# Attention and rational-activation FFN on one core: q and k of later units transposed with unrounded float32r bits and split after PSUM

## The chip, the cores and the metric

The kernel runs on one core of a Trainium2 chip. Its time is the device time of one execution in microseconds (us); a figure for a kernel is the median of several executions.

## The reference

Inputs: q, k and v of 4 batches, 8 heads, 768 positions, head size 64, all float32; weights w_in (512 x 2048) and w_out (2048 x 512); two small coefficient vectors a and b. Attention keeps the keys of a causal local window (`n_local` = 96) and the first `n_global` = 8 keys, with a linear distance bias per head; the output of the heads, 3072 tokens by 512, goes through a feed-forward layer with a rational activation.

```python
scores = scale * np.matmul(q, k.transpose(0, 1, 3, 2))
is_global = pos[None, :] < int(n_global)
is_local = (rel >= 0) & (rel < int(n_local))
keep = is_global | is_local
dist = np.where(is_global & ~is_local, float(n_local), np.abs(rel))
scores = np.where(keep, scores - slopes[:, None, None] * dist, -1e9)
a = softmax(scores);  attn = np.matmul(a, v)
...
h = x @ w_in
P = a[0] + a[1] * h + a[2] * h**2 + a[3] * h**3
Q = 1.0 + np.abs(b[0]) * np.abs(h) + np.abs(b[1]) * h**2
out = (P / (Q + 1e-06)) @ w_out
```

## The kernel before, in words

**Units and steps.** The work is cut into 96 units. A unit is one pair of heads of one tile of 128 queries; a chunk is 256 tokens (two tiles, eight units), and there are 12 chunks. `windowed` (L506) writes out a pipeline over steps t, 110 in all. At step t it emits, each with a priority (`PRI`, L42): the load of q, k and v for two units at every even step (`st_load`, L127), the transposes of unit t (`st_qkT`, L373), their eviction (`st_qkE`, L385), the split of unit t + 1 (`st_split`, L365), scores, softmax, normalization and copy of unit t - 2 (`st_score` L400, `st_soft` L424, `st_norm` L436, `st_raw` L446), the transposes of the probabilities of unit t - 3 (`st_pT`, L455), the product with v for a pair of units (`st_pv`, L468), and the feed-forward work of the slice that lies `LAG` = 12 steps back, its second product another `F2` = 2 steps later (`st_ffn1` L242, `st_ew1` to `st_ew4` L274 to L314, `st_ffn2` L320). In the first twenty-odd steps the weights are decoded from their 64-bit containers and split as well (`WSCHED`, `SPLITS`). A scheduler then puts each engine's instructions in a fixed order, by priority and by a simulated time of when each could run. On the chip each engine works through its list strictly in that order.

**Float32r products in parts.** The matmuls of the feed-forward layer and of the scores run in float32r, which keeps fewer bits, so each operand is split into a high part (rounded) and a low part (what rounding left). The feed-forward product of a slice takes three matmuls (high by high, high by low, low by high), on L258 and L334.

**q and k before the change.** A pair of units shares one tile `nat` of q and k (128 positions; 4 heads of 64). For a unit, `st_split` makes a tile `sp` with, for each head, the 64 high columns beside the 64 low columns: VectorE rounds (L369), GpSimd subtracts (L370). `st_qkT` transposes it on TensorE: four transposes of 128x128 (q and k, two heads) into one PSUM tile `tk` (L378), which after that has the high part of a head on partitions 0 to 63 and the low part on 64 to 127. `st_qkE` evicts it on ScalarE: q of each head with its scale (L392), k into the lasting tile `kT` (L395), for the first tile of a sequence also the global keys into `kG` (L397). Two DMAs on SyncE's queue copy q with the halves swapped (L393, L394), so that two matmuls per head (L408) sum all four products of parts.

**Queues and buffers.** All DMAs are issued by SyncE (SP), in order. The PSUM tiles of the transposes, the scores and the product with v (`tk`, `s`, `tp`, `o`) share one pool of three buffers. From unit `RAW` = 30 on, the normalized probabilities are copied by a DMA into a float32r tile with their bits unrounded (L452) and transposed in that form (L462); before unit 30 they are transposed as float32. The copy has one buffer.

The functions that the change touches:

Of the kernel before, what the change touches and what calls it, by code (L numbers as in the profile page):

```python
# [9 lines left out]
F32 = mybir.dt.float32  # L10
FR = mybir.dt.float32r
I32 = mybir.dt.int32
U16 = mybir.dt.uint16
AF = mybir.ActivationFunctionType
ALU = mybir.AluOpType
PSUM = bass.MemoryType.PSUM

P = 128
G = 8
# [3 lines left out]
TMPS = 6  # L23
GBUFS = 3
RAW = 30
LAG = 12
F2 = 2

# [67 lines left out]
def tile_kernel(ctx: ExitStack, tc: tile.TileContext, q, k, v, n_global, n_local,  # L96
                w_in, w_out, ca, cb, out):
    nc = tc.nc
    B, H, S, D = q.shape
# [15 lines left out]
    pl = SimpleNamespace(tmps=TMPS, gbufs=GBUFS, split=False)  # L115


    nat = {}
    vts = {}

    def unit(u):
        c, j = divmod(u, UPC)
        t, p = divmod(j, NPAIR)
        b, i = divmod(2 * c + t, NT)
        return c, t, p, b, i
# [81 lines left out]
    def split_w(key):  # L207
        low[key] = piece(FR, key)
        (nc.vector.tensor_copy if len(low) - 1 in HI_V else nc.scalar.copy)(out=w_hi(key), in_=full[key])
        (nc.vector if len(low) - 1 in LO_V else nc.gpsimd).tensor_tensor(  # L210
            out=low[key], in0=full[key], in1=w_hi(key), op=ALU.subtract)
# [137 lines left out]
    kT = const.tile([P, H, 2, P], FR, name="kT")  # L349
    kG = const.tile([P, H, G], FR, name="kG")  # L350
    ident = const.tile([P, P], F32, name="ident")
    ident_r = const.tile([P, P], FR, name="ident_r")
    mask0 = const.tile([P, P], F32, name="mask0")
    masks = const.tile([P, 3, P], F32, name="masks")
    sp = {}
    tqk = {}
    qTs = {}
# [4 lines left out]
    def blocks_of(x, i):  # L362
        return x if i else x[..., 0, :]

    def st_split(u):  # L365
        p = unit(u)[2]
        n = nat[u // 2][:, :, 2 * (p % 2):2 * (p % 2) + 2, :]
        s = pl.att.tile([P, 2, 2, 2, D], FR, tag="split", name=f"sp{u}", bufs=1)
        nc.vector.tensor_copy(out=s[:, :, :, 0, :], in_=n)  # L369
        nc.gpsimd.tensor_tensor(out=s[:, :, :, 1, :], in0=n, in1=s[:, :, :, 0, :], op=ALU.subtract)  # L370
        sp[u] = s

    def st_qkT(u):  # L373
        s = sp.pop(u)
        tk = pl.ps_t.tile([P, 2, 2, P], FR, tag="t", name=f"tk{u}")
        for z in range(2):
            for x in range(2):
                nc.tensor.transpose(out=tk[:, z, x, :], in_=s[:, z, x].rearrange("p a d -> p (a d)"),  # L378
                                    identity=ident_r)
        tqk[u] = tk  # L380
# [4 lines left out]
    def st_qkE(u):  # L385
        c, t, p, b, i = unit(u)
        tk = tqk.pop(u)
        hs = slice(2 * p, 2 * p + 2)
        qT = pl.att.tile([P, 2, 2, P], FR, tag="qT", name=f"qT{u}")
        for x in range(2):  # L390

            nc.scalar.activation(out=qT[:, 0, x], in_=tk[:, 0, x], func=AF.Copy, scale=float(2.0 ** (2 * p + x - 2)))  # L392
        nc.sync.dma_start(out=qT[0:D, 1].bitcast(F32), in_=qT[D:P, 0].bitcast(F32))  # L393
        nc.sync.dma_start(out=qT[D:P, 1].bitcast(F32), in_=qT[0:D, 0].bitcast(F32))  # L394
        nc.scalar.copy(out=kT[:, hs, i % 2, :], in_=tk[:, 1])  # L395
        if i == 0:
            nc.scalar.copy(out=kG[:, hs, :], in_=tk[:, 1, :, 0:G])  # L397
        qTs[u] = qT

    def st_score(u):  # L400
        c, t, p, b, i = unit(u)
        qT = qTs.pop(u)
        s_ps = pl.ps_t.tile([P, 2, 2, P], F32, tag="t", name=f"s{u}")
        for x in range(2):
            h = 2 * p + x
            rhs = kT[:, h] if i else kT[:, h, 0:1, :].broadcast_to([P, 2, P])
            for z in range(2):
                nc.tensor.matmul(out=s_ps[:, x], lhsT=qT[:, z, x, :], rhs=rhs, start=(z == 0), stop=(z == 1))  # L408
        if 1 <= i < NT - 1:
            nc.gpsimd.tensor_copy(out=kT[:, 2 * p:2 * p + 2, i % 2, 0:G], in_=kG[:, 2 * p:2 * p + 2, :])  # L410
        if i == 0:
            mk = mask0
        else:
            mk = masks[:, 0:2, :] if i % 2 else masks[:, 1:3, :]
        pr = pl.att.tile([P, 2, 2, P], F32, tag="prob", name=f"pr{u}")
        st = stats[:, u % 4]
        for x in range(2):
            h = 2 * p + x
            nc.vector.tensor_tensor_reduce(  # L419
                out=blocks_of(pr[:, x], i), in0=blocks_of(s_ps[:, x], i), in1=mk,  # L420
                scale=-(2.0 ** -(h + 1)), scalar=3e38, op0=ALU.add, op1=ALU.min, accum_out=st[:, x:x + 1])
        prob[u] = (pr, st)
# [23 lines left out]
    def st_raw(u):  # L446
        if u < RAW:
            return
        i = unit(u)[4]
        pr = prob[u][0]  # L450
        raw = pl.att.tile([P, 2, 2, P], FR, tag="raw", name=f"raw{u}", bufs=1)
        nc.sync.dma_start(out=blocks_of(raw.bitcast(F32), i), in_=blocks_of(pr, i))  # L452
        prob[u] = (raw, None)

    def st_pT(u):  # L455
        i = unit(u)[4]
        pr, st = prob.pop(u)
        W = 2 if i else 1
        t_ps = pl.ps_t.tile([P, 2, 2, P], FR if u >= RAW else F32, tag="t", name=f"tp{u}")
        for x in range(2):  # L460
            for w in range(W):
                nc.tensor.transpose(out=t_ps[:, x, w, :], in_=pr[:, x, w, :], identity=ident_r if u >= RAW else ident)  # L462
        pT = pl.att.tile([P, 2, 2, P], F32, tag="pT", name=f"pT{u}", bufs=2)
        t_ps = t_ps.bitcast(F32) if u >= RAW else t_ps
        (nc.scalar.copy if u < EARLY else nc.vector.tensor_copy)(out=pT[:, :, 0:W, :], in_=t_ps[:, :, 0:W, :])  # L465
# [40 lines left out]
    def windowed():  # L506
# [6 lines left out]
        nc.vector.tensor_copy(out=nf, in_=ni)  # L513
        load_coef()
        st_split(0)
        st_split(1)

        nl, ng = nf[:, 0:1], nf[:, 2:3]
# [4 lines left out]
        base = tc.cur_priority  # L523
        for t in range(NU + LAG + F2):
            f = t - LAG
            pri = PRI_A if f < FPC else PRI
# [9 lines left out]
            on("soft", st_soft, t - 2)  # L536
            on("ffn1a", st_ffn1, f, 0)
            on("qkT", st_qkT, t)
            if t % 2:
                on("pv", lambda u: st_pv(u // 2), t - 5)  # L540
            on("qkE", st_qkE, t)
            if t % 2:
                on("x", lambda u: st_x(u // 2), t - 5)
            if t:
                on("split", st_split, t + 1)
            if not is_last(f - 1):
                on("ew3", st_ew3, f - 1)
            on("norm", st_norm, t - 2)
            on("raw", st_raw, t - 2)
            if is_last(f):  # L550
                st_ew4(f - 1)
# [15 lines left out]
            for n, key in enumerate(list(full)[SPLITS.get(f - 1, 0):SPLITS.get(f, 0)]):  # L567
                tc.cur_priority = base + 1000 * t + pri["wsplit"] + 4 * n
                split_w(key)
        tc.cur_priority = base + 1000 * (NU + LAG + F2 + 4)  # L570

# [153 lines left out]
```

## Time and profile before

| | us |
|---|---|
| median of 3 runs | 794.35 |
| lowest, highest | 793.64, 794.79 |
| the profiled execution | 792.2 |
| its span, first to last instruction | 790.4 |

| engine | busy us | share of span |
|---|---|---|
| TensorE (PE), matmuls | 743.9 | 94% |
| TensorE, weight loads (PEld) | 649.6 | 82% |
| VectorE (DVE) | 599.6 | 76% |
| ScalarE (ACT) | 575.1 | 73% |
| GpSimd (POOL) | 533.3 | 67% |

In the profile, a row of a group of instructions has the line of the kernel, the engine and the operation; then the tile that is written `<-` the tiles that are read, the shape and the count; behind the first bar the busy time in us and the mean duration of one in ns; behind the second bar the idle time of that engine just before them, and what ended it. `PEld` is the load of weights for a matmul, which overlaps the matmul before it; `SPq` is SyncE's DMA queue. The page's digits show each of 40 equal slices of the span in tenths. Rows of a timeline or a chain begin with the start and the length in us.

### The profile page before, as it was taken

The page shows a single profiled execution, that of the slowest core. Times are in us where ns is not written, and L with a number is a line of the kernel's source. Part 1 is how long each engine was busy: PE and PEld are TensorE (multiplying, and loading weights), DVE is VectorE, ACT ScalarE, POOL GpSimd, SP SyncE. Part 2 cuts the span into 40 slices and gives each one's busy share as a digit, 9 for nine tenths or more (in the row PEclk, how much of TensorE's full clock was granted, in tenths as well). Part 3 has the DMA queues.
Part 4 walks back from the last instruction along what each step waited for, and adds up shares of the span by engine and source line. Part 5 has one row for each costly group of instructions (what it writes and reads, how often), then busy time and mean ns, then how long its engine had stood idle before and what let it go on. Part 6 is the DMA issues. An engine that isn't in the chain of part 4 may idle for free.

```text
span 790.4 us, 15799 instructions
## 1 busy us (share of the span) xinstructions
PE 743.9 (94%) x5184; PEld 649.6 (82%) x5184; DVE 599.6 (76%) x1453; ACT 575.1 (73%) x1407; POOL 533.3 (67%) x572
## 2 busy tenths in 40 slices
PE   3688978899999999999999999999999999999995
PEld 2467647688998899999899999989999999988993
DVE  5889999987778676777776786777677786776664
ACT  4778677667887777777777777777877777766763
POOL 3868558979877667666667667666677777664440
PEclk9999999899999999999999999999999999999999
DMA  7785445212222233333332332333332332210000
GB/s 183 212 240 173 114 125 189 49 48 54 55 81 68 85 92 87 97 88 86 82 87 82 106 84 81 106 84 82 88 85 77 101 92 78 82 55 14 28 1 32
DMA packets 111932, 72.19 MB, mean 91 GB/s; under 512 B 82912, under 2 KB 97248, under 8 KB 111840
## 3 DMA queue, kind: packets, MB, share of 16 engines
q1 hardware_dynamic: 111840, 71.08, 32.0%
q8 instruction: 44, 0.72, 0.4%
q14 instruction: 48, 0.39, 0.2%
HBM read 35.92 MB, written 6.29 MB: 53 GB/s over the span
## 4 chain that ended last, share of the span: by engine, by line
PE 81%; DVE 6%; POOL 5%; DMA 4%; issue 2%; ACT 1%; SPq 0%; DVEq 0%; POOLq 0%; ACTq 0%
PE h L258 32%; PE acc L334 31%; PE o L480 5%; PE s L408 5%; PE tp L462 3%; PE tk L378 3%; DMA r<-in_moe_w_in_dram 2%; POOL pr L441 2%; PE h L250 1%; POOL sp L370 1%; DMA nat<-in_k_dram 1%; POOL fa L291 1%; DVE pr L419 1%; DVE fu L305 0%; DMA r<-in_moe_w_out_dram 0%
## 5 line engine op out<-in xcount | busy, mean ns | idle before, releaser
L334 PE MATMUL acc<-wout_h,g 128*128 128x512 f32 x704 | 242.8, 403 | 0.8 <-ACT g L313 0.8
L258 PE MATMUL h<-xh,win_h 128*128 128x256 f32 x704 | 205.4, 292 | 1.8 <-DVE fu L290 1.8
L441 POOL TENSOR_SCALAR pr<-pr,stats 128x256 f32<-128x256 f32 (+1 forms) x192 | 178.5, 940 | 39.2 <-issue 12.7
L258 PE MATMUL h<-xl,win_h 128*128 128x256 f32 x704 | 198.7, 282 | 0.0
L291 POOL TENSOR_TENSOR fa<-fa,fs 128x512 f32<-128x512 f32 x95 | 125.1, 1317 | 100.7 <-ACT fs L284 97.4
L334 PEld LDWEIGHTS acc<-wout_h,g 128*128 128x128 f32 x704 | 126.6, 188 | 21.8 <-ACT g L313 1.2
L258 PEld LDWEIGHTS h<-xh,win_h 128*128 128x128 f32 x704 | 133.3, 189 | 10.9 <-issue 6.2
L258 PEld LDWEIGHTS h<-xl,win_h 128*128 128x128 f32 x704 | 133.3, 189 | 2.3 <-issue 0.2
L429 ACT ACTIVATE pr<-pr,stats 128x256 f32<-128x256 f32 (+1 forms) x192 | 93.5, 492 | 53.5 <-DVE stats L419 53.4
L370 POOL TENSOR_TENSOR sp<-nat,sp 128x256 fp32r<-128x256 f32 x96 | 75.8, 790 | 73.5 <-DVE stats L432 41.0
L314 POOL TENSOR_TENSOR g<-fu,g 128x512 fp32r<-128x512 f32 x87 | 112.7, 1295 | 7.7 <-DVE fu L290 4.6
L282 ACT ACTIVATE fu<-h,coef 128x512 f32<-128x512 f32 (+1 forms) x97 | 75.4, 778 | 54.1 <-PE h L258 49.6
L303 DVE SCALAR_TENSOR_TENSOR fu<-fu,coef,q 128x512 f32<-128x512 f32 (+1 forms) x97 | 71.6, 738 | 36.2 <-ACT q L299 35.0
L298 ACT ACTIVATE fs<-fa,coef 128x512 f32<-128x512 f32 (+1 forms) x97 | 70.2, 724 | 30.3 <-POOL fa L291 27.9
L289 DVE TENSOR_TENSOR fu<-fu,h 128x512 f32<-128x512 f32 (+1 forms) x97 | 65.6, 677 | 16.9 <-ACT fs L284 14.9
L465 DVE COPY pT<-tp 128x512 f32<-128x512 f32 (+1 forms) x75 | 48.5, 646 | 35.7 <-PE tp L462 35.0
L369 DVE CAST sp<-nat 128x256 fp32r<-128x256 f32 x96 | 38.3, 399 | 46.7 <-PE tk L378 15.1
L290 DVE SCALAR_TENSOR_TENSOR fu<-fu,coef,h 128x512 f32<-128x512 f32 (+1 forms) x97 | 71.7, 739 | 2.5
L419 DVE CUSTOM_DVE_ANT_0 pr<-s,masks 128x256 f32<-128x256 f32 x160 | 61.4, 420 | 15.2 <-PE s L408 13.3
L408 PE MATMUL s<-kT,qT 128*128 128x256 f32 x384 | 70.5, 305 | 1.8 <-DMA qT<-qT 1.7
L304 DVE SCALAR_TENSOR_TENSOR q<-fa,coef,q 128x512 f32<-128x512 f32 (+1 forms) x97 | 72.1, 744 | 0.0
L408 PEld LDWEIGHTS s<-kT,qT 128*128 128x128 f32 x384 | 61.5, 203 | 9.0 <-DMA qT<-qT 1.9
(273 smaller groups left out, 1658.8 us busy)
## 6 DMA issues: line engine op xcount, KB each, us to landing
raw<-pr SPq DMA_DIRECT2D x58, 256.0 KB
qT<-qT SPq DMA_DIRECT2D x192, 64.0 KB
r<-in_moe_w_in_dram SPq DMA_DIRECT2D x16, 512.0 KB
r<-in_moe_w_out_dram SPq DMA_DIRECT2D x16, 512.0 KB
nat<-in_q_dram SPq DMA_DIRECT2D x48, 128.0 KB
nat<-in_k_dram SPq DMA_DIRECT2D x48, 128.0 KB
vt<-in_v_dram SPq DMA_DIRECT2D x48, 128.0 KB
out_dram<-o SPq DMA_DIRECT2D x24, 256.0 KB
```

The costliest lines, as they stand in the source:

```text
L258: nc.tensor.matmul(out=hps[f][:, y, :], lhsT=w[:, fs], rhs=x[:, ct, :], start=(n == 0), stop=(n == 3 * NCT - 1))
L282: nc.scalar.activation(out=u, in_=h, func=AF.Identity, scale=a3, bias=a2)
L290: nc.vector.scalar_tensor_tensor(out=u, in0=u, scalar=a1, in1=h, op0=ALU.add, op1=ALU.mult)
L291: side(f).tensor_tensor(out=a, in0=a, in1=s, op=ALU.add)
L303: nc.vector.scalar_tensor_tensor(out=u, in0=u, scalar=a0, in1=r, op0=ALU.add, op1=ALU.mult)
L304: nc.vector.scalar_tensor_tensor(out=r, in0=a, scalar=q1, in1=r, op0=ALU.add, op1=ALU.mult)
L314: side(f).tensor_tensor(out=g[:, 1, ys], in0=u, in1=g[:, 0, ys], op=ALU.subtract)
L334: nc.tensor.matmul(out=acc, lhsT=gs[f][:, z, y, ts], rhs=w, start=(ft == 0 and n == 0), stop=(ft == NFT - 1 and n == 2))
L370: nc.gpsimd.tensor_tensor(out=s[:, :, :, 1, :], in0=n, in1=s[:, :, :, 0, :], op=ALU.subtract)
L408: nc.tensor.matmul(out=s_ps[:, x], lhsT=qT[:, z, x, :], rhs=rhs, start=(z == 0), stop=(z == 1))
L429: nc.scalar.activation(out=d, in_=d, func=AF.Exp, scale=-1.0, bias=st[:, x:x + 1], accum_out=st[:, 2 + 2 * x:3 + 2 * x])
L441: nc.gpsimd.tensor_scalar(out=d, in0=d, scalar1=st[:, 6 + x:7 + x], scalar2=None, op0=ALU.mult)
```

## The change

For units from the 24th on (`RAWQ` = 24; unit 24 is the first of the second batch) the split moves behind the transposes.

- `st_split` no longer rounds and subtracts. At every second unit one DMA on SyncE's queue copies the natural q and k of two units (256 KB) into a float32r tile, bits unrounded, with two buffers.
- `st_qkT` makes two transposes instead of four: one of q and one of k, each with both heads of the unit side by side. One head then lies on partitions 0 to 63 of `tk` and the other on 64 to 127.
- `raw_qkE`, new, evicts and splits. ScalarE writes the high parts of q (scaled) and of k, 64 partitions at a time, four activations in place of three. VectorE subtracts these from PSUM for the low parts, four operations, of which those of k go to a small tile `kl`. Four DMAs on SyncE's queue per unit copy q's parts to the other half of the partitions, and the low part of k into the other half of `kT`.
- The global keys (`kG`, once per sequence and pair of heads) are copied by GpSimd from `kT`, after the DMA, and no longer by ScalarE from PSUM.
- The scores are the same instructions; their two matmuls per head sum the same four products in another arrangement.
- The copy of the probabilities (`raw`) has two buffers instead of one, and the SBUF that is set aside for dynamic DMAs is set to 2048 bytes.

```diff
+RAWQ = 24
...
     def st_split(u):
         p = unit(u)[2]
+        if u >= RAWQ:
+
+            if u % 2 == 0:
+                s = pl.att.tile([P, 2, 4, D], FR, tag="rawq", name=f"sp{u}", bufs=2)
+                nc.sync.dma_start(out=s.bitcast(F32), in_=nat[u // 2])
+                sp[u] = sp[u + 1] = s
+            return
...
     def st_qkT(u):
         s = sp.pop(u)
+        if u >= RAWQ:
+            p = unit(u)[2]
+            tk = pl.ps_t.tile([P, 2, P], FR, tag="t", name=f"tk{u}")
+            for z in range(2):
+                nc.tensor.transpose(out=tk[:, z, :], in_=s[:, z, 2 * (p % 2):2 * (p % 2) + 2].rearrange("p a d -> p (a d)"),
+                                    identity=ident_r)
+            tqk[u] = tk.bitcast(F32)
+            return
...
         qT = pl.att.tile([P, 2, 2, P], FR, tag="qT", name=f"qT{u}")
+        if u >= RAWQ:
+            raw_qkE(p, i, tk, qT)
+            qTs[u] = qT
+            return
...
+    def raw_qkE(p, i, tk, qT):
+        kl = pl.att.tile([P, P], FR, tag="kl", name="kl", bufs=2)
+        rows = (slice(0, D), slice(D, P))
+        for x in range(2):
+            own, h = rows[x], 2 * p + x
+            scale = float(2.0 ** (h - 2))
+            nc.scalar.activation(out=qT[own, 0, x], in_=tk[own, 0], func=AF.Copy, scale=scale)
+            nc.scalar.copy(out=kT[own, h, i % 2, :], in_=tk[own, 1])
+        for x in range(2):
+            own, other, h = rows[x], rows[1 - x], 2 * p + x
+            scale = float(2.0 ** (h - 2))
+            nc.vector.scalar_tensor_tensor(out=qT[own, 1, x], in0=tk[own, 0], scalar=scale, in1=qT[own, 0, x],
+                                           op0=ALU.mult, op1=ALU.subtract)
+            nc.vector.tensor_tensor(out=kl[own], in0=tk[own, 1], in1=kT[own, h, i % 2, :], op=ALU.subtract)
+            nc.sync.dma_start(out=qT[other, :, x].bitcast(F32), in_=qT[own, :, x].bitcast(F32))
+            nc.sync.dma_start(out=kT[other, h, i % 2, :].bitcast(F32), in_=kl[own].bitcast(F32))
+        if i == 0:
+            nc.gpsimd.tensor_copy(out=kG[:, 2 * p:2 * p + 2, :], in_=kT[:, 2 * p:2 * p + 2, 0, 0:G])
...
-        raw = pl.att.tile([P, 2, 2, P], FR, tag="raw", name=f"raw{u}", bufs=1)
+        raw = pl.att.tile([P, 2, 2, P], FR, tag="raw", name=f"raw{u}", bufs=2)
...
-    nc = _bacc.Bacc("TRN2", target_bir_lowering=False, num_devices=1)
+    nc = _bacc.Bacc("TRN2", target_bir_lowering=False, num_devices=1, dynamic_dma_scratch_size=2048)
```

## The prediction

> **What bounds the kernel now.** I read four views in this order: the page's digits per slice, the busy time by stage, the chain of work within the steady stage, and the waits there.
>
> ```profile
> PE   3688978899999999999999999999999999999995
> DVE  5889999987778676777776786777677786776664
> PEclk9999999899999999999999999999999999999999
> ```
>
> TensorE is full from about the ninth slice (20 us each) to the end, at full clock; VectorE is full before that and at six to eight tenths afterwards. The busy time by stage gives the edges:
>
> ```profile
> core 0: us, PE busy (x) PEld busy (x) DVE busy (x) ACT busy (x) POOL busy (x), PEclk, DMA share, GB/s
> 120.00:160.00 40.00, 34.50 (x197) 26.45 (x196) 38.95 (x83) 29.27 (x70) 36.76 (x30) 0.91 0.36 105
> 160.00:230.00 70.00, 70.00 (x508) 62.52 (x507) 55.45 (x129) 52.68 (x134) 58.70 (x60) 1.00 0.23 58
> 230.00:690.00 460.00, 460.00 (x3440) 415.62 (x3438) 340.20 (x841) 349.34 (x864) 320.98 (x357) 1.00 0.31 87
> 690.00:760.00 70.00, 70.00 (x491) 63.11 (x490) 46.31 (x84) 48.51 (x92) 36.01 (x31) 1.00 0.09 29
> ```
>
> From 160 to 760 us TensorE is busy without a gap. Its ends are modelled, so the next view matters more: the chain in 230 to 690 us by line, and all that TensorE's weight loads waited for there.
>
> ```profile
> by line: PE h L258 40.4%; PE acc L334 39.0%; PE o L480 6.6%; PE s L408 6.5%; PE tk L378 3.9%; PE tp L462 3.6%
> PEld h L258 <- issue: 5.1, 30, 0.2
> PEld o L480 <- issue: 0.7, 2, 0.4
> PEld tp L462 <- issue: 0.2, 1, 0.2
> PEld acc L334 <- issue: 0.2, 1, 0.2
> PEld acc L334 <- POOL g L314: 0.2, 1, 0.2
> ```
>
> The six shares add to 100%: the chain in this stage is TensorE alone. It waited 6.4 us of 460, and 0.2 us of that for another engine. So here the time is the sum of what TensorE's instructions take, and an instruction taken from it shortens the run by its own pitch as long as all others keep up. The unit work of the steady stage repeats about every 7.4 us (460 us with some 62 units, by the rows of L432 and L370 below).
>
> **TensorE's term.** For units 24 to 95 the transposes of q and k (L378) fall from four to two a unit, of the same 128x128 shape. What one costs is not its mean duration, since they overlap, but the step in the chain:
>
> ```profile
> 309.74 0.12 PE tp L462 x2
> 314.35 0.30 PE tk L378 x4
> 317.75 0.29 PE tp L462 x4
> ```
>
> Runs of four take 0.30 and 0.29 us, a run of two 0.12 us; L462 is the transpose of the probabilities, which already goes through float32r with unrounded bits. So two fewer save 0.17 to 0.18 us; I take 0.175. Units 24 to 95 are 72: 72 x 0.175 = 12.6 us, 2.4% of a unit's 7.4 us. All of them lie in the full part: unit 29 is transposed just before 210.80 (its row is below), and L378 ends before 700 us. The row above gives nearly the same from the other side: 3.9% of 460 us is 17.9 us, 0.29 us for each of 62 units, of which a bit over half goes.
>
> [...]
>
> **VectorE, ScalarE, GpSimd.** These cost nothing as long as TensorE is fed, so I work out how full each becomes. All rows are of 230 to 690 us.
>
> ```profile
> L369 DVE CAST sp<-nat 128x256 fp32r<-128x256 f32 x61 | 22.6, 370 | 38.5 <-PE tk L378 10.2 <-POOL kT L410 9.1 <-issue 7.8
> L500 DVE TENSOR_TENSOR xl<-o,xh 128x256 fp32r<-128x256 f32 x31 | 13.1, 421 | 10.1 <-ACT xh L499 10.0
> L432 DVE TENSOR_REDUCE stats<-stats 128x2 f32<-128x4 f32 x62 | 9.3, 150 | 2.8 <-ACT pr L429 2.6
> L419 DVE CUSTOM_DVE_ANT_0 pr<-s,mask 128x128 f32<-128x128 f32 x16 | 4.0, 289 | 0.8 <-PE s L408 0.7
> L370 POOL TENSOR_TENSOR sp<-nat,sp 128x256 fp32r<-128x256 f32 x62 | 45.8, 738 | 53.9 <-DVE stats L432 41.0 <-DVE sp L369 12.6
> L392 ACT ACTIVATE qT<-tk 128x128 fp32r<-128x128 f32 x122 | 26.3, 264 | 2.5 <-PE tk L378 1.5
> L395 ACT CAST kT<-tk 128x256 fp32r<-128x256 f32 x61 | 22.5, 370 | 0.0
> ```
>
> VectorE loses the cast of L369 (370 ns) and gains four operations of 64 partitions by 128 elements, with one operand in PSUM. The trace has no such form. Below lies nothing cheaper than half the 256-wide subtraction of L500 (210 ns), above it L500 itself (421 ns); nearest is the 128-wide L419, which also reads PSUM and a tile in SBUF: 289 ns. Four are 1.16 us, less 0.37: +0.79 us a unit, between +0.47 and +1.31. VectorE is busy 340.2 us in 62 units, 5.49 us each; it becomes 6.28 us of 7.23, 87%.
>
> [...]
>
> ScalarE goes from 2 x 264 + 370 = 898 ns to four activations of 128 elements, 4 x 264 = 1056 ns: +0.16 us on 349.34 / 62 = 5.63 us, 80% of 7.23. GpSimd loses 0.74 us a unit; the copy of kG at a sequence's first tile moves to it from ScalarE (12 units, small). It has the most room of all.
>
> **SyncE's queue and the longer way to the scores.** Two DMAs of low parts of k a unit and one copy of q and k per two units are added to the queue, in order with everything else:
>
> ```profile
> L393 SPq DMA_DIRECT2D qT<-qT x96: 461/467/912, 6.6 to 697.7; - x96
> L394 SPq DMA_DIRECT2D qT<-qT x96: 461/588/1420, 8.4 to 698.7; - x96
> L452 SPq DMA_DIRECT2D raw<-pr x66: 465/478/1574, 233.3 to 715.5; - x66
> ```
>
> At 0.48 to 0.59 us each, 2.5 more are 1.2 to 1.5 us of issue a unit in a queue that issues some 2.3 us today (these three, and the loads at about half a microsecond each). Half the queue's time stays free. The four DMAs of a unit now wait for VectorE; behind them stand the copy of the probabilities (L452) and the loads. What becomes late first would be the scores. Their lead over the last ScalarE row of the same unit, in a usual and in the shortest case of the 72:
>
> ```profile
> 402.86 0.38 ACT L395 CAST kT<-tk 128x256 fp32r<-128x256 f32 x1
> 414.86 0.40 PE L408 MATMUL s<-kT,qT 128*128 128x256 f32 x2
> 211.13 0.38 ACT L395 CAST kT<-tk 128x256 fp32r<-128x256 f32 x1
> 218.19 0.52 PE L408 MATMUL s<-kT,qT 128*128 128x256 f32 x3
> 210.80 0.45 ACT L392 ACTIVATE qT<-tk 128x128 fp32r<-128x128 f32 x2 [1.34 <-PE tk L378]
> 1.23 2.86 DMA nat<-in_k_dram
> ```
>
> 11.6 us, and 6.7 us at the least. The new steps are 1.16 us on VectorE, some waiting for its turn, and a DMA; the only landing near it in size that the chain shows is 2.86 us for 128 KB from memory. Some 5 us together: hidden in the steady stage, tight at units 27 to 29. The copy of q and k takes the place of 0.37 + 0.74 us of cast and subtraction, with a lead of several us before L378. The second buffer of the copied probabilities can only free the queue; the smaller scratch I cost at nothing, as no GpSimd DMA queue is on the page.
>
> Between 160 and 230 us VectorE is at 55.45 of 70 us and still has weight splits; 9 units x 0.79 us bring it to 62.6. Were it on the path for units 24 to 27, it would cost 4 x 0.79 = 3.2 us; at best nothing. I take 1.0 us.
>
> **The sum.** The profiled execution took 792.2 us, 790.4 of it span: 792.2 - 12.6 + 1.0 = 780.6 us. The median of the runs lies 2.15 us higher, 794.35 us: 782.8 us is forecast for it. A difference within 0.2% (1.6 us) counts as no change; a measurement here can't tell less.
>
> **Rivals.**
> 1. *Part of the gain is eaten.* The new waits (scores behind the low parts' DMAs, the PSUM tile of the transposes held until VectorE has read it) stop TensorE now and then. At 0.05 to 0.175 us a unit, 3.6 to 12.6 us come back: 786 to 795 us, most likely 790. For it: three buffers serve all transposes and scores. Against: the leads above.
> 2. *VectorE becomes the bound: slower.* It is idle 119.8 us in the stage, 1.93 us a unit, waiting in its order for others. If that idle time does not shrink, a unit takes 5.49 + 0.79 + 1.93 = 8.2 us: +57 us, 851 us. It decides from the point where more than 7.4 - 6.28 = 1.12 us of idle time a unit remains; with 1.2 us a unit takes 7.48 us, +5.8 us, 800 us, the value I give it. For it: strict order, and TensorE fell to 34.50 of 40 us where VectorE was full (120 to 160 us). Against: in that stage VectorE's idle time was 1.05 us of 40, so it does shrink when work is queued.
> 3. *The unrounded bits take the slow way.* The transposes of fp32 before unit 30 took 0.22 us for two:
>
> ```profile
> 234.46 0.22 PE tp L462 x2
> ```
>
> Then a unit saves 0.30 - 0.22 = 0.08 us: 5.8 us, 789.6 us with the 1.0 above. Against: L462 with unrounded bits runs at 0.12 for two.
>
> **Numbers.** Forecast 0.70, rival 1 0.16, rival 2 0.10, rival 3 0.04. A quarter of rival 1's stretch lies within 1.6 us of 794.35: same 0.04; slower 0.10 is rival 2; faster 0.70 + 0.12 + 0.04 = 0.86. The low end is 778.5: the whole 12.6 us and about half of the 6.4 us of small waits, which a changed order may take away. The high end is 790.5: 0.05 us a unit kept (3.6 us). Between them lie the forecast, rival 3 and half of rival 1, 0.82 in all.
>
> **What would show it.** Right: L378 with 240 transposes (24 x 4 + 72 x 2), runs of two at about 0.12 us in the chain, a steady chain still all TensorE, units every 7.2 us, VectorE near 87% and GpSimd near 60% there, four new VectorE rows at 250 to 300 ns. Wrong: waits of TensorE for the DMAs into kT or qT, for VectorE at the transposes' tile, or a steady chain with VectorE or SyncE in it; or runs of two that take over 0.2 us.

## The result, and the profile after

| | us |
|---|---|
| after: median of 8 runs (lowest, highest) | 786.78 (784.15, 790.85) |
| before, beside it: median of 8 runs (lowest, highest) | 794.03 (792.01, 797.16) |
| after : before, 95% interval | 0.9907 [0.9883, 0.9931] |
| the profiled execution of after | 788.42 |
| its span | 786.6 |

The kernel is faster by 7.4 us (0.9%), between 5.5 and 9.3 by the interval. 11.6 us had been forecast. One execution of e4_qkE_late (1412 us) and one of the kernel before (896 us) lie far outside all others and are left out of the ratios. The page's digits per slice, after:

```profile
PE   3678988899999999999999999999999999999995
DVE  5888998989878887878778789788788688776664
PEclk9998999899999999999999999999999999999999
```

TensorE is still full from the ninth slice on. VectorE has moved up by about a tenth. The busy time by stage of after, in the first three of the stretches that were shown of before (the first row names the columns: length, then busy time and count of each engine, granted clock, DMA share, rate):

```profile
core 0: us, PE busy (x) PEld busy (x) DVE busy (x) ACT busy (x) POOL busy (x), PEclk, DMA share, GB/s
120.00:160.00 40.00, 34.43 (x202) 27.20 (x201) 37.83 (x77) 27.88 (x68) 34.06 (x29) 0.87 0.45 130
160.00:230.00 70.00, 68.60 (x477) 59.70 (x476) 59.20 (x153) 53.86 (x134) 50.16 (x53) 1.00 0.29 77
230.00:690.00 460.00, 458.57 (x3377) 411.53 (x3375) 375.61 (x1040) 366.51 (x931) 280.62 (x308) 1.00 0.41 113
```

TensorE, without a gap before, now has 1.40 us of gaps in 160 to 230 us and 1.43 us in 230 to 690 us. VectorE went from 340.20 to 375.61 us in the long stage, ScalarE from 349.34 to 366.51, GpSimd from 320.98 to 280.62. The waits of TensorE in 165 to 700 us of after (in all, how often, the longest; the same view of before has no row at all):

```profile
PE h L259 <- DVE fu L291: 1.5, 3, 1.0
PE tk L387 <- DVE xl L542: 1.1, 1, 1.1
PE s L450 <- PE tp L504: 0.3, 1, 0.3
```

The prediction had read the bound from what TensorE's weight loads waited for in 230 to 690 us: 6.4 us, of which 0.2 for another engine. In after they wait 12.6 us there, of which 5.5 for VectorE, in these rows:

```profile
PEld h L259 <- DVE fu L291: 2.2, 2, 1.4
PEld o L522 <- DVE stats L474: 1.0, 3, 0.4
PEld o L522 <- DVE kl L436: 0.7, 2, 0.4
PEld o L522 <- DVE fu L291: 0.7, 2, 0.4
PEld tp L504 <- DVE fu L291: 0.5, 1, 0.5
PEld o L522 <- DVE qT L434: 0.4, 1, 0.4
```

The chain of work in 230 to 690 us of after by line, as far as the view gives it:

```profile
by line: PE h L259 36.7%; PE acc L335 35.3%; PE s L450 6.6%; PE o L522 5.5%; PE tp L504 3.6%; PE tk L387 1.6%; ACT pr L471 1.3%; issue 1.0%; ACT fa L284 0.8%; ACT fu L283 0.8%; ACT q L300 0.6%; ACT fs L299 0.6%; DMA out_dram<-o 0.6%; ACT fs
```

Two pieces of the chain in 300 to 330 us of after:

```profile
308.12 0.30 PE tp L504 x4
308.96 0.13 PE tk L387 x2
```

The transposes of q and k (tk) fell from 3.9% to 1.6%, and a run of two takes 0.13 us (0.12 in others) where a run of four still takes 0.30. TensorE's rows add to 89.3%, no longer to 100%. The remaining tenth is not time lost: TensorE had gaps of 1.43 us in 460. Where it waits once, the chain turns off to the engine that it waited for and runs back along that engine's list, beside a TensorE that is working, until it meets TensorE again. A few short waits are enough to colour a chain so.

**A measure that the start leaves alone.** By the profiled executions after is 788.42 against 792.2 us, only 3.8 us less. To see where, I take the start of the first matmul of the feed-forward layer in slice 12 and in slice 92, two fixed places in the list of TensorE, 80 units apart. Timeline of before:

```profile
170.60 0.28 PE L258 MATMUL h<-xh,win_h 128*128 128x256 f32 x1
750.42 0.28 PE L258 MATMUL h<-xh,win_h 128*128 128x256 f32 x1
```

Timeline of after:

```profile
173.18 0.28 PE L259 MATMUL h<-xh,win_h 128*128 128x256 f32 x1
746.40 0.28 PE L259 MATMUL h<-xh,win_h 128*128 128x256 f32 x1
```

Between the marks before took 579.8 us and after 573.2: 6.6 us less. Ahead of the first mark TensorE's list is the same in both, and after came to it 2.6 us later. Behind the second, to the end of the span, they took 40.0 and 40.2 us. So -6.6 + 2.6 + 0.2 gives the 3.8 us. The 2.6 us are most likely the clock and not the change. The busy rows of after and then of before for 7 us each, both ahead of the first mark:

```profile
67.00:74.00 7.00, 6.02 (x14) 4.79 (x15) 6.84 (x17) 7.00 (x20) 4.56 (x4) 0.51 0.53 143
```

```profile
150.00:157.00 7.00, 6.10 (x27) 5.70 (x28) 7.00 (x18) 4.62 (x14) 6.91 (x6) 0.51 0.25 57
```

The granted clock was 0.51 there. Stretches of 3.4 or 6.8 us of this kind came to 10.2 us in the profiled execution of before and to 20.5 in that of after, at other places in each. Twelve kernels of this document (all but e10_qkT_later and e12_both) have the same list of TensorE up to the mark. Those with the least such time (6.8 us, e8_dma2 and e9_no_low) reach the mark at 168.12 and 169.46 us, that with the most (23.9 us, e6_dve2) at 175.21. It is not the clock alone, since with 13.7 us of it the mark lies anywhere between 171.30 and 174.06. From 160 us to the second mark the clock is 1.00 in before and after. I call the time between the two marks "the stage" below, and use it beside the medians: it comes from one execution, but the start does not disturb it. In three of the experiments a stretch at half clock lies inside the stage: at 191 us in e6_dve2, at 189 and 534 us in e7_dve4, at 192 us in e10_qkT_later, each 3.4 us at a granted clock of 0.5. There matmuls into h start every 0.21 us in place of 0.12. By the steps within them these stretches make the stages 1.9, 3.1 and 1.5 us longer, and the tables give the stage without that.

### The profile page after: what moved, and what is told of

Same layout as the page of the kernel before. It is cut to its first block, busy times and chain, and to the rows that moved or that the text cites. A ratio compares the mean times of both kernels' runs of the same rounds, so it can differ in the third digit from the quotient of the medians.

```text
span 786.6 us, 16348 instructions
## 1 busy us (share of the span) xinstructions
PE 735.9 (94%) x5040; PEld 636.9 (81%) x5040; DVE 636.1 (81%) x1669; ACT 588.3 (75%) x1467; POOL 480.1 (61%) x512
## 4 chain that ended last, share of the span: by engine, by line
PE 73%; DVE 9%; DMA 5%; ACT 5%; POOL 4%; issue 3%; SPq 0%; DVEq 0%; POOLq 0%; ACTq 0%
PE h L259 29%; PE acc L335 28%; PE s L450 5%; PE o L522 4%; PE tp L504 3%; POOL pr L483 2%; DMA r<-in_moe_w_in_dram 2%; PE acc L330 2%; PE h L251 1%; DMA r<-in_moe_w_out_dram 1%; PE tk L387 1%; ACT pr L471 1%; DVE pr L461 1%; DVE q L305 1%; DVE fu L290 1%
## 5 line engine op out<-in xcount | busy, mean ns | idle before, releaser
L335 PE MATMUL acc<-wout_h,g 128*128 128x512 f32 x704 | 242.0, 402 | 1.2 <-ACT g L314 1.1
L259 PE MATMUL h<-xh,win_h 128*128 128x256 f32 x704 | 202.7, 288 | 3.3 <-DVE fu L291 3.3
L335 PEld LDWEIGHTS acc<-wout_h,g 128*128 128x128 f32 x704 | 126.6, 188 | 24.3 <-issue 3.3
L471 ACT ACTIVATE pr<-pr,stats 128x256 f32<-128x256 f32 (+1 forms) x192 | 93.2, 490 | 14.6 <-DVE stats L461 13.7
L290 DVE TENSOR_TENSOR fu<-fu,h 128x512 f32<-128x512 f32 (+1 forms) x97 | 65.6, 676 | 16.3 <-ACT fs L285 15.5
L450 PE MATMUL s<-kT,qT 128*128 128x256 f32 x384 | 73.1, 311 | 2.6 <-DMA qT<-qT 2.3
L291 DVE SCALAR_TENSOR_TENSOR fu<-fu,coef,h 128x512 f32<-128x512 f32 (+1 forms) x97 | 71.5, 737 | 1.2
L314 ACT CAST g<-fu 128x512 fp32r<-128x512 f32 (+1 forms) x89 | 54.8, 616 | 17.9 <-DVE fu L306 17.5
L306 DVE SCALAR_TENSOR_TENSOR fu<-q,fu 128x512 f32<-128x512 f32 (+1 forms) x97 | 66.1, 681 | 1.1
L285 ACT ACTIVATE fs<-h,coef 128x512 f32<-128x512 f32 (+1 forms) x97 | 66.4, 685 | 0.7
```

What stands on the lines that cost most here:

```text
L259: nc.tensor.matmul(out=hps[f][:, y, :], lhsT=w[:, fs], rhs=x[:, ct, :], start=(n == 0), stop=(n == 3 * NCT - 1))
L290: nc.vector.tensor_tensor(out=u, in0=u, in1=h, op=ALU.mult)
L291: nc.vector.scalar_tensor_tensor(out=u, in0=u, scalar=a1, in1=h, op0=ALU.add, op1=ALU.mult)
L335: nc.tensor.matmul(out=acc, lhsT=gs[f][:, z, y, ts], rhs=w, start=(ft == 0 and n == 0), stop=(ft == NFT - 1 and n == 2))
L471: nc.scalar.activation(out=d, in_=d, func=AF.Exp, scale=-1.0, bias=st[:, x:x + 1], accum_out=st[:, 2 + 2 * x:3 + 2 * x])
```

## The experiments

Two theories were put to the test. A: the transposes brought what was forecast, and the rest of the change (four VectorE operations, four DMAs, four activations a unit, new waits) took some of it back. B: on the path a transpose is worth less than its step in the chain, and the rest costs next to nothing. In the tables "waits" is worked out from the start times of TensorE's matmuls within the stage: each step from one start to the next that exceeds the median step between the same two kinds of matmul, with the same kinds just before and behind them, by 60 ns or more counts with its excess (0.2 us for before, 4.9 for after). A kind is the tile that is written, the medians are over all kernels, and steps at half clock are left out. This is more than the waits view shows (1.5 + 1.1 + 0.3 = 2.9 us for after in 165 to 700 us), since the row of a matmul is longer than its step to the next start (0.39 against 0.23 us at L335 from 402.27 us in after) and covers the first part of a wait. "List" is the stage less the waits: what TensorE's instructions take in their order. Which neighbours are compared moves both by some 0.7 us.

One thing holds for all experiments but e2_rawbuf: the scheduler works again for every edit, and TensorE's list comes out in another order. A kernel shows its edit together with that new order, and "list" helps to tell the two apart. In before the list takes 579.6 us and in after 568.3, 11.3 less; the waits went from 0.2 to 4.9, 4.7 more. That is the 6.6 us.

### Four transposes again (e1_tr4)

Everything of the change stays, but each of the two transposes is made twice, into a tile of double size of which one half is used.

```diff
-            tk = pl.ps_t.tile([P, 2, P], FR, tag="t", name=f"tk{u}")
+            tk = pl.ps_t.tile([P, 2, 2, P], FR, tag="t", name=f"tk{u}")
             for z in range(2):
-                nc.tensor.transpose(out=tk[:, z, :], in_=s[:, z, 2 * (p % 2):2 * (p % 2) + 2].rearrange("p a d -> p (a d)"),
-                                    identity=ident_r)
+                for x in range(2):
+                    nc.tensor.transpose(out=tk[:, z, x, :],
+                                        in_=s[:, z, 2 * (p % 2):2 * (p % 2) + 2].rearrange("p a d -> p (a d)"),
+                                        identity=ident_r)
-            tqk[u] = tk.bitcast(F32)
+            tqk[u] = tk[:, :, 0, :].bitcast(F32)
```

> The changed kernel with each of the two transposes of a unit issued twice (the second copy goes to an unused half of the PSUM tile), so that TensorE again has four a unit; all else of the change stays. Theory A (the transposes taken away are worth their pitch in the chain, 12.6 us, and 5 us of that is given back by the rest of the change): about 799 us, 12 us over the changed kernel and 5 us over the kernel before. Rival B (the transposes are worth only what was gained, about 7 us, and the rest of the change is free): 794 us, level with the kernel before.

Measured: 799.67 us, 1.005 [1.003, 1.007] of before. The marks in its timeline:

```profile
174.72 0.28 PE L259 MATMUL h<-xh,win_h 128*128 128x256 f32 x1
759.25 0.28 PE L259 MATMUL h<-xh,win_h 128*128 128x256 f32 x1
```

The stage is 584.5 us: 11.3 longer than after's, 4.7 longer than before's; 4.0 us of waits, and a list of 580.5. So two transposes fewer are worth 11.3 us by the stage, 12.2 by the list (580.5 - 568.3), 12.9 by the medians (799.67 - 786.78), 11.4 by the ratios ((1.005 - 0.9907) x 794). The 799 us of theory A came; B falls: the transposes bring 11 to 13 us, and all the rest of the change costs 4.0 us [2.4, 5.6] by this kernel's ratio, 4.7 by the stage. Of the 4.7, 3.8 are waits (4.0 against 0.2) and 0.9 is the list (580.5 against 579.6), with as many matmuls in another order.

### The side edits alone (e2_rawbuf)

Before, with the second buffer for the copied probabilities and the smaller setting for dynamic DMAs.

```diff
-        raw = pl.att.tile([P, 2, 2, P], FR, tag="raw", name=f"raw{u}", bufs=1)
+        raw = pl.att.tile([P, 2, 2, P], FR, tag="raw", name=f"raw{u}", bufs=2)
-    nc = _bacc.Bacc("TRN2", target_bir_lowering=False, num_devices=1)
+    nc = _bacc.Bacc("TRN2", target_bir_lowering=False, num_devices=1, dynamic_dma_scratch_size=2048)
```

> The kernel before with only the two side edits: two buffers for the copied probabilities, and the smaller SBUF reserve for dynamic DMAs. Both theories: level with the kernel before, 794 us within 1 us, and TensorE's list unchanged. If these edits carry part of the gain, it is 2 us or more faster.

Measured: 794.99 us, 0.9999 [0.9978, 1.002]; stage 579.8 us as before, TensorE's list the same. The two edits by themselves cost and bring nothing.

### A later start (e3_rawq32)

```diff
-RAWQ = 24
+RAWQ = 32
```

> The changed kernel with the new way from unit 32 on and not 24, so that it begins after the weight splits. 8 units lose 0.175 us each, 1.4 us. Theory A with an early cost (TensorE's waits at 186 to 189 us, where VectorE is full, are 1.8 us of what is lost): level with the changed kernel or up to 1 us faster. Rival (the loss is spread evenly over all units): 0.8 to 1.4 us slower than the changed kernel, 788 us.

Measured: 789.81 us, 0.9936 [0.9915, 0.9957]; stage 574.0, waits 3.3. Eight units without the change cost 8 x 0.157 us (11.3 / 72) = 1.3 us; by the stage 0.8 came, as the rival had it, by the ratios 2.3, by the medians 3.0, which neither theory had. In 160 to 230 us TensorE has no gap any more, and in the long stage it has what after had:

```profile
160.00:230.00 70.00, 70.00 (x511) 62.90 (x510) 54.43 (x131) 52.94 (x136) 56.21 (x57) 1.00 0.29 73
230.00:690.00 460.00, 458.49 (x3372) 408.70 (x3370) 376.91 (x1041) 366.63 (x928) 279.38 (x305) 1.00 0.41 113
```

So the units beside the weight splits are not where most of the 4.7 us goes: of after's 4.9 us of waits 3.3 are still there. Most of the loss is spread over the stage.

### Evictions with a lower priority (e4_qkE_late)

```diff
-qkE=300
+qkE=720
```

> The changed kernel with the eviction of q and k placed behind the elementwise work of the feed-forward slice in the scheduler's priorities (720 in place of 300). Theory A1 (TensorE waits because the four new VectorE operations stand ahead of the operation that frees the feed-forward PSUM tile, as at 402.5 us): those waits go, 1 to 3 us faster than the changed kernel, 784 to 786 us. Rival (the loss is not in those waits but in the order of TensorE's own list): within 1 us of the changed kernel.

Measured: 789.8 us, 0.9924 [0.9896, 0.9952]; stage 575.0, waits 6.1. Faster by 1 to 3 us was expected of theory A1, and it is not: 1.8 us slower by the stage. The two longest waits of TensorE in 165 to 700 us in this kernel:

```profile
PE acc L335 <- POOL g L315: 2.4, 2, 1.2
PE tk L387 <- DVE xl L542: 1.1, 1, 1.1
```

The wait for fu is gone, and new ones for g, at the other end of the feed-forward slice, are longer. That the place of the evictions in the order makes the loss is not borne out: another place moves the waits.

### VectorE with less to do (e5_no_klow, e9_no_low)

e5_no_klow leaves out the low part of k: its two operations a unit are gone, and the DMA carries the high part in its place.

```diff
-            nc.vector.tensor_tensor(out=kl[own], in0=tk[own, 1], in1=kT[own, h, i % 2, :], op=ALU.subtract)
-            nc.sync.dma_start(out=kT[other, h, i % 2, :].bitcast(F32), in_=kl[own].bitcast(F32))
+            nc.sync.dma_start(out=kT[other, h, i % 2, :].bitcast(F32), in_=kT[own, h, i % 2, :].bitcast(F32))
```

> The changed kernel without the two VectorE operations a unit that make the low part of k; the DMA that carries it is kept and carries the high part in its place, so this kernel leaves out the low part of k. Theory V (what is given back is TensorE waiting for a VectorE that comes late): VectorE is relieved of some 0.5 us a unit, half of its new work, and about half of the 5 us comes back: 2 to 3 us faster than the changed kernel, 784 us. Rival S (SyncE's longer queue and the DMAs on the way to the scores cost it): as many DMAs as before, so within 1 us of the changed kernel.

e9_no_low leaves out the low part of q as well, so that VectorE has none of the four operations; the DMAs of q carry half, and the second matmul of the scores repeats the first one's q.

```diff
-            nc.vector.scalar_tensor_tensor(out=qT[own, 1, x], in0=tk[own, 0], scalar=scale, in1=qT[own, 0, x],
-                                           op0=ALU.mult, op1=ALU.subtract)
-            nc.sync.dma_start(out=qT[other, :, x].bitcast(F32), in_=qT[own, :, x].bitcast(F32))
+            nc.sync.dma_start(out=qT[other, 0, x].bitcast(F32), in_=qT[own, 0, x].bitcast(F32))
...
-                nc.tensor.matmul(out=s_ps[:, x], lhsT=qT[:, z, x, :], rhs=rhs, start=(z == 0), stop=(z == 1))
+                nc.tensor.matmul(out=s_ps[:, x], lhsT=qT[:, 0 if u >= RAWQ else z, x, :], rhs=rhs, start=(z == 0), stop=(z == 1))
```

> The changed kernel without any of the four new VectorE operations; the DMAs stay (those of q carry half the bytes) and wait for ScalarE alone. It leaves out the low parts of q and k, and the second score matmul of a head repeats the first's operand; as many matmuls. Theory V (TensorE waits because VectorE comes late): VectorE is a little below its load in the kernel before, TensorE's waits between 160 and 690 us shrink from some 3 us of idle time (by the windows) to under 1, and the time is 2 to 4 us below the changed kernel, 783 to 785 us. Rival S (the DMAs and SyncE's queue): no change within 1 us. In both, some 1.5 us that the new order of TensorE's list costs stays.

| | median | ratio to before | stage | waits | list |
|---|---|---|---|---|---|
| after | 786.78 | 0.9907 [0.9883, 0.9931] | 573.2 | 4.9 | 568.3 |
| e5_no_klow | 786.68 | 0.9908 [0.9877, 0.994] | 571.4 | 2.3 | 569.1 |
| e9_no_low | 785.78 | 0.9903 [0.9873, 0.9934] | 571.8 | 1.3 | 570.5 |

In the long stage VectorE, the third pair of numbers, falls by 17 us in e5_no_klow and by 52 in e9_no_low, there to less than it had before the change. First e5_no_klow, then e9_no_low:

```profile
230.00:690.00 460.00, 459.33 (x3372) 412.61 (x3371) 358.27 (x919) 370.12 (x933) 279.88 (x308) 1.00 0.41 113
```

```profile
230.00:690.00 460.00, 459.02 (x3377) 412.76 (x3376) 323.27 (x790) 369.08 (x931) 279.25 (x306) 1.00 0.36 104
```

The waits fall to a half and to a quarter, and the weight loads' waits for VectorE in 230 to 690 us from 5.5 us to 2.5 and 1.4. So most of the new waits go with the new operations; in e9_no_low TensorE's gaps in 160 to 690 us shrink from 2.8 us to 1.0, as theory V expected. The time does not follow. Theory V expected 2 to 3 and 2 to 4 us less; the stage is 1.8 and 1.4 us shorter, and the medians and ratios can't tell that from nothing, which is what rival S expected. By the list this is the new order: it takes 0.8 and 2.2 us longer with as many matmuls, and eats a good part of what the waits give back.

### VectorE with more to do (e6_dve2, e7_dve4)

The operation that makes the low part of k is issued twice and three times: two and four more a unit.

```diff
             nc.vector.tensor_tensor(out=kl[own], in0=tk[own, 1], in1=kT[own, h, i % 2, :], op=ALU.subtract)
+            nc.vector.tensor_tensor(out=kl[own], in0=tk[own, 1], in1=kT[own, h, i % 2, :], op=ALU.subtract)
```

> The changed kernel with the low part of k computed twice: two more VectorE operations a unit (six in place of four), with the same result. Theory V: VectorE goes from 82% to about 88% of the steady stage, TensorE's waits grow by about as much as the four cost before or more: 2 to 5 us slower than the changed kernel, 789 to 792 us. Rival S: within 1 us.

> The changed kernel with the low part of k computed three times: four more VectorE operations a unit (eight in place of four), with the same result. Theory V: VectorE at about 95%, past the point where its idle time is enough; 8 to 20 us slower than the changed kernel, at or above the kernel before. Rival S: within 1 us.

| | median | ratio to before | stage | waits | list | VectorE idle in 230 to 690 us |
|---|---|---|---|---|---|---|
| before | 794.03 | | 579.8 | 0.2 | 579.6 | 119.8 |
| after | 786.78 | 0.9907 [0.9883, 0.9931] | 573.2 | 4.9 | 568.3 | 84.4 |
| e6_dve2 | 804.98 | 1.0142 [1.0103, 1.0181] | 585.2 | 16.8 | 568.4 | 58.0 |
| e7_dve4 | 816.78 | 1.0295 [1.0256, 1.0334] | 599.5 | 30.9 | 568.6 | 39.2 |

The long stage of e6_dve2, and behind it that of e7_dve4:

```profile
230.00:690.00 460.00, 450.85 (x3289) 401.69 (x3288) 401.99 (x1142) 358.64 (x906) 275.24 (x302) 1.00 0.41 112
```

```profile
230.00:690.00 460.00, 441.15 (x3184) 390.39 (x3183) 420.81 (x1225) 348.82 (x883) 267.91 (x293) 1.00 0.39 108
```

Two operations more cost 12.0 us of stage, four 26.3: 0.17 and 0.37 us a unit for 72 units, where each pair puts 2 x 0.28 = 0.56 us on VectorE. Nearly all of it is waits; the list stays. 2 to 5 and 8 to 20 us had been expected of theory V: its direction came, its size was too small. Down from after the same pair was worth 1.8 us of stage and the next one nothing. There is an edge, and after stands just short of it. At 402 of 460 us (87%) VectorE is still idle for an eighth of it, and the two operations more already cost as much as the transposes brought. The waits of e7_dve4, in 165 to 700 us:

```profile
PE acc L335 <- ACT g L314: 4.8, 5, 1.5
PE tp L506 <- DMA raw<-pr: 4.0, 2, 3.8
PE o L524 <- DVE stats L463: 3.1, 3, 1.5
PE tp L506 <- DVE xl L544: 2.9, 1, 2.9
PE h L259 <- DVE fu L291: 2.2, 4, 1.2
PE tk L387 <- DVE kl L438: 1.6, 3, 0.9
PE s L452 <- DMA kT<-kl: 0.8, 2, 0.6
```

The waits are in many places where something has passed through VectorE, also where the releaser named is ScalarE's or a DMA. The new operations themselves (kl) are named in 2.4 of the 19.4 us of these rows. That the rest is what stands behind them in VectorE's list is likely, but not shown.

### The DMA of the low part of k twice (e8_dma2)

```diff
             nc.sync.dma_start(out=kT[other, h, i % 2, :].bitcast(F32), in_=kl[own].bitcast(F32))
+            nc.sync.dma_start(out=kT[other, h, i % 2, :].bitcast(F32), in_=kl[own].bitcast(F32))
```

> The changed kernel with each DMA of the low part of k issued twice: two more DMAs a unit, some 1.1 us more of issue in SyncE's queue and 64 KB more moved. Theory V: within 1 us of the changed kernel. Rival S: 2 us slower or more.

Measured: 789.08 us, 0.9941 [0.9918, 0.9965]; stage 575.5 (after 573.2), waits 7.1. Two DMAs more a unit are 2.3 us slower by the stage and by the medians: that is what rival S had named and not theory V, but the intervals overlap. The DMAs of the change by themselves can't be the main cause of the waits, since e9_no_low keeps all of them (those of q with half the bytes) and has 1.3 us of waits left. That SyncE's queue is free is not shown.

### Another place for the transposes, and a reduction less (e10_qkT_later, e11_no_reduce, e12_both)

e10_qkT_later moves the transposes of a unit later in the order. e11_no_reduce takes a VectorE operation away: from unit 24 on the reciprocals of the softmax are taken of the sums directly, without the reduction that adds 1e-9 to them. e12_both has both.

```diff
-qkT=200
+qkT=270
```

```diff
+            if u >= RAWQ:
+                nc.vector.reciprocal(out=st[:, 6:8], in_=st[:, 2:6:2])
+                return
```

> The changed kernel with the transposes of q and k placed behind the product with v in the scheduler's priorities (270 in place of 200). TensorE's list then has, with each neighbour pair at the pitch that it has in the two profiles, 1.8 us less in the same matmuls. If the order of the list is what costs part of the loss: 1 to 2 us faster than the changed kernel, 785 us. If the waits decide: within 1 us, with the waits at other places.

> The changed kernel without the VectorE reduction that adds 1e-9 to the softmax sums, from unit 24 on (the sums are 1 or more, where float32 does not hold 1e-9); one VectorE operation of 150 ns less a unit, and one link less from the softmax to the normalization. Theory V: a third of what leaving out two of the new operations brings, 0.5 to 1 us faster than the changed kernel, 786 us. Rival S: no change.

> The two before it together, as a version that might beat both kernels: 1.5 to 3 us faster than the changed kernel, 784 to 785 us, if both effects hold and add; within 1 us of it if they do not.

| | median | ratio to before | stage | waits | list |
|---|---|---|---|---|---|
| after | 786.78 | 0.9907 [0.9883, 0.9931] | 573.2 | 4.9 | 568.3 |
| e10_qkT_later | 789.89 | 0.9951 [0.9925, 0.9978] | 574.9 | 6.0 | 568.9 |
| e11_no_reduce | 786.39 | 0.9895 [0.9868, 0.9921] | 570.8 | 2.7 | 568.1 |
| e12_both | 789.2 | 0.9934 [0.9909, 0.9958] | 573.9 | 5.1 | 568.8 |

The later place was expected to bring 1 to 2 us, and the list to shrink by 1.8. It costs 1.7 us of stage with the reduction and 3.1 without it, mostly waits, and the list does not shrink. Without the reduction (0.15 us a unit) the stage is 2.4 and 1.0 us shorter, mostly waits too, but the medians differ by 0.4 and 0.7 us only (0.5 to 1 us had been expected). The 784 to 785 us of e12_both did not come. e11_no_reduce has the shortest stage of all kernels and beats before; that it beats after can't be said, since the intervals overlap. No kernel here beats both clearly.

## Why the prediction was right or wrong, point by point

**The bound and the transposes' term: right.** TensorE's list is the path, and what was taken from it came off the time: 12.6 us were forecast, 11.3 (stage) to 12.9 (medians) measured by e1_tr4. By the stage a transpose is worth 11.3 / 144 = 78 ns, by the list 12.2 / 144 = 85, by the medians 90. Instructions and steps are as forecast: 144 transposes at L387 and 96 at L394, runs of two at 0.12 to 0.13 us. Rival 3, the slow way for unrounded bits, falls with these rows: it would have shown runs of 0.22 us.

**The step that failed: "at best nothing. I take 1.0 us".** That term was to hold all that the rest of the change costs. It measured 4.0 us [2.4, 5.6], or 4.7 by the stage. I had looked for it beside the weight splits only, at units 24 to 27, and costed the steady stage at nothing, "hidden". e3_rawq32 shows that most of it is spread over the steady stage. Of the 11.6 us forecast, 6.6 came by the stage. Of the 5.0 that are missing, 3.7 are waits of TensorE: 4.7 more than before, where 1.0 stood for everything. The other 1.3 are the list, 11.3 us shorter where 12.6 was forecast; e1_tr4 puts 0.4 of that down to the transposes (12.2) and 0.9 to the new order, which the forecast did not cost at all. The total stayed within the range because its upper end left room for all but 3.6 us of the gain to go.

**Rival 1: its mechanism took place beside the forecast's, near the lower end of its price.** 4.0 to 4.7 us over 72 units are 0.056 to 0.065 us a unit, where 0.05 to 0.175 stood. The places that it named were only half right. The scores behind the DMAs of the low parts did not turn up among after's waits in 165 to 700 us. What did, in the longest wait, is the feed-forward layer, held up on VectorE. Timelines of after, VectorE first:

```profile
401.46 0.68 DVE L290 TENSOR_TENSOR fu<-fu,h 128x512 f32<-128x512 f32 x1
402.05 0.28 DVE L434 SCALAR_TENSOR_TENSOR qT<-tk,qT 64x128 fp32r<-64x128 f32 x1
402.25 0.28 DVE L436 TENSOR_TENSOR kl<-tk,kT 64x128 fp32r<-64x128 f32 x1
402.56 0.29 DVE L434 SCALAR_TENSOR_TENSOR qT<-tk,qT 64x128 fp32r<-64x128 f32 x1
402.77 0.29 DVE L436 TENSOR_TENSOR kl<-tk,kT 64x128 fp32r<-64x128 f32 x1
403.09 0.75 DVE L291 SCALAR_TENSOR_TENSOR fu<-fu,coef,h 128x512 f32<-128x512 f32 x1
```

```profile
402.50 0.40 PE L335 MATMUL acc<-wout_h,g 128*128 128x512 f32 x1
403.89 0.39 PE L259 MATMUL h<-xh,win_h 128*128 128x256 f32 x1 [1.00 <-DVE fu L291]
```

L290 and L291 are two steps of one feed-forward slice. The four new operations stand between them in VectorE's list, so L291 starts at 403.09 where L434 started at 402.05, a delay of about 1.04 us. L291 is the last reader of h in PSUM, and TensorE's next matmul into h waited 1.00 us for it. This wait is 1.0 of the 4.9 us; for most of the others the cause is not shown. The transposes' tile, the second place, shows in one wait of 1.1 us. VectorE's list just before the transposes that waited, which began at 188.66:

```profile
186.79 0.69 DVE L211 TENSOR_TENSOR w_3l<-w_3f,win_h 128x512 fp32r<-128x512 f32 x1
187.40 0.15 DVE L474 TENSOR_REDUCE stats<-stats 128x2 f32<-128x4 f32 x1
187.58 0.69 DVE L306 SCALAR_TENSOR_TENSOR fu<-q,fu 128x512 f32<-128x512 f32 x1
188.19 0.41 DVE L542 TENSOR_TENSOR xl<-o,xh 128x256 fp32r<-128x256 f32 x1
```

The transposes waited for a buffer of the shared PSUM pool. Its reader, L542, stood behind three other operations of VectorE, one of them a weight split.

**VectorE's load: each operation right, the sum too high, and what follows from it wrong.** The rows of after by form in 230 to 690 us (busy time and mean ns of one; then idle time before them):

```profile
L434 DVE SCALAR_TENSOR_TENSOR qT<-tk,qT 64x128 fp32r<-64x128 f32 x126 | 36.0, 286 | 17.2 <-ACT kT L430 14.7
L436 DVE TENSOR_TENSOR kl<-tk,kT 64x128 fp32r<-64x128 f32 x126 | 35.2, 279 | 0.0
```

279 and 286 ns were measured where 289 was forecast from L419. But operations overlap at their ends, as the timeline shows (four in 1.04 us, not 1.16): over the stretch the durations of VectorE's rows add to 379 us before and 430 after, 39 and 55 us more than its busy time, which is 55 / 64.2 - 39 / 63.4 = 0.24 us of overlap a unit more. And the unit count of 62 was low: 80 units in 579.8 us are 7.25 us each, 63.4 in 460 us (64.2 after, at 573.2 / 80 = 7.165). With that VectorE went from 340.20 / 63.4 = 5.37 us a unit to 375.61 / 64.2 = 5.85 us: +0.48 instead of +0.79, 82% instead of 87%. ScalarE (366.51 of 460, 80%) and GpSimd (280.62, 61%) came out as forecast. So the reason was not that VectorE is fuller than thought. The forecast asked how full an engine becomes; the list asks what stands in front of whom.

**SyncE's queue: at the forecast's upper end.** The new DMAs in the tile view of after (least, median and longest duration of the issue, ns):

```profile
L437 SPq DMA_DIRECT2D qT<-qT x144: 591/618/1577, 179.8 to 694.9; - x144
L438 SPq DMA_DIRECT2D kT<-kl x144: 462/555/2050, 180.6 to 695.6; - x144
```

555 ns at the median for the low part of k lies within the forecast's 0.48 to 0.59 us; 618 for q, where 467 and 588 stood, lies above it. With half a copy of q and k at 478 ns that is 2 x 0.555 + 0.24 + 0.18 = 1.53 us a unit more, where 1.2 to 1.5 was forecast. What they cost TensorE is not settled (e8_dma2). The side edits at nothing: right, by e2_rawbuf.

**Rival 2, VectorE as the bound: it was nearer than 0.10 let it seem.** VectorE's idle time per unit was 119.8 / 63.4 = 1.9 us before, 84.4 / 64.2 = 1.3 after, 58.0 / 62.9 = 0.9 in e6_dve2 and 39.2 / 61.4 = 0.6 in e7_dve4 (units by each kernel's stage). The idle time does shrink when work is queued, which was the argument against the rival; but TensorE pays while it shrinks. Two operations more a unit, 0.56 us, end slower than before.

**Still open.** Of the 4.7 us that the rest of the change costs, 3.8 are waits in e1_tr4 and 0.9 is the new order of TensorE's list. That most of the waits hang on VectorE is borne out three times: without the new operations 1.3 of 4.9 us stay, with two more they are 16.8, with four more 30.9. It is not shown which places make up the 4.9 us, nor what the DMAs have in it. No edit gave the time back: e5_no_klow and e9_no_low lost by the new order part of what they gained by fewer waits, and a kernel that changes the order alone (e4_qkE_late, e10_qkT_later) has more waits.

## What to carry to other kernels

Where one engine is the path, take the price of an instruction from its step in the chain, not from its mean duration, and trust it: here the forecast and the experiment agree within 1.3 us of 12.6. Then look at the cover not by its load but by its order: for each operation that is added to an engine's list, find the operation that stands right behind it and who waits for that one (here L291, about 1.04 us late, and a matmul into h that waited 1.00 us), and give this a price of its own. Test the edge by adding some more of the same work once (here half as much again): the distance to the point where it tips says more than the busy share. And where a scheduler orders the lists, look whether an experiment that takes one thing away has also changed the order of the engine that is the path, before its time is put down to that one thing.

## What the runs showed of the hardware

- TensorE, full itself, lost time to VectorE long before VectorE was full: with VectorE busy for 74% of 230 to 690 us TensorE's waits in the stage were 0.2 us (before), at 82% 4.9 (after), at 87% 16.8 (e6_dve2) and at 91% 30.9 (e7_dve4). The busy share alone does not set them: in e9_no_low it was 70%, and 1.3 us of waits were there.
- The same list of TensorE reached the same matmul at 170.60 us in one execution and at 173.18 in another, with 10.2 and 20.5 us at a granted clock of about 0.51 on the way, in pieces of 3.4 us or twice that. The 2.6 us of scatter between these two executions are a third of what the change brought.
- Transposes of float32r with unrounded bits ran at the rate of rounded ones: runs of four in 0.29 us against 0.30 (the rows of the prediction) and runs of two in 0.12 to 0.13 us, where those of float32 took 0.22.
